# A recurrent attention and gated feed-forward kernel: conversions of the output weight queued behind the last masks and copies of part 1, leftover gate tiles in another form, and a fold's parts reordered

## The chip, the cores and the metric

The kernel runs on one core of a Trainium2 chip. The core has a matrix engine (TensorE, "PE" in the profile, with its weight loads listed apart as "PEld"), a vector engine (VectorE, "DVE"), a scalar engine (ScalarE, "ACT"), GpSimd ("POOL") and SyncE ("SP"), which here only issues DMA transfers. Each engine takes its own instructions strictly in order; they wait for each other through semaphores. The metric is the device time of one launch in microseconds. Before the change it is 488.24 us, the median of 4 runs (486.95 to 489.95). A difference under 0.5% (2.4 us) can't be told from no change with such runs.

## What is computed

The reference, cut to what matters: a gated linear attention over 4 batches, 8 heads, 768 steps and 48 values a head, and a feed-forward block on its output, where two projections are multiplied with each other.

```python
state = zeros((B, H, D, D)); y = zeros_like(q)
for t in range(S):
    state = alpha[:, :, t, :, None] * state + einsum('bhd,bhe->bhde', k[:, :, t], v[:, :, t])
    y[:, :, t] = einsum('bhd,bhde->bhe', q[:, :, t], state)
x = y.transpose(0, 2, 1, 3).reshape(B * S, H * D)      # 3072 x 384
a, b = x @ w1, x @ w2                                  # 384 -> 1024 each
out = (a * b @ w3) @ w_out                             # 1024 -> 1024 -> 384
```

The four weights arrive as 64-bit floating point, the four attention inputs and the result are 32-bit.

## The kernel before

**Part 1, the attention.** The sequence is cut into 24 chunks of 128 steps (`N = 24`), and the loop `for n in range(N + 1)` (line 568) handles one chunk in each turn, with its parts spread over neighbouring turns: decays (`logs`, `decays`), scaled and transposed queries and keys (`transposed`, whose copies out of PSUM are line 306 on ACT), the scores of a chunk and their causal mask (`scores`; the mask is line 347, two DVE instructions a chunk), the product with the carried state (`attend_state`, line 363), the product with the values (`attend`, line 369, with two ACT copies of the result in line 373), and the chunk's own outer product (`outer`, line 316 with a DVE addition in line 326). The result of a chunk goes to a buffer in HBM, `xd`, by the stores of line 241. Three chunks make a group of 384 columns; there are 8 groups.

**Gate tiles, which fill the matrix engine.** For a group `g` and a block `f` of 128 of the 1024 columns, `gate` computes both projections and multiplies them. Each number is split into three parts, so that one factor takes nine matmuls of 128x384: six of parts 0 and 1 into one PSUM bank, three of part 2. The group's input is fetched by `load_x` (line 384) and split into three parts by `split_x` (line 390 on ACT, lines 391 and 392 on DVE). There are two forms of a gate. The early form (`gate`, through `exact`) uses two banks for a factor, an ACT scaling (line 407) and a DVE combination (line 409), and a DVE product (line 445): for a tile two ACT and three DVE instructions. The late form (`late_gate`, through `onto`) uses one bank for a factor: six matmuls, an ACT scaling in place (line 422), and the last three matmuls on top of it, which `settle(2)` holds back until two more factors have begun; ACT then brings one factor out (line 454) and DVE multiplies (line 458): three ACT instructions and one DVE instruction for a tile. A tile's result is stored by line 469. The 24 early tiles of groups 0 to 4 are put into a list, `fill`, and handed out between the parts of the attention; those that part 1 leaves over are taken first by the second loop.

**Conversion of the weights.** `to_fp32` fetches one tile of raw 64-bit words by DMA (line 183, three buffers) and makes 32-bit numbers of it: on ACT lines 191 and 196, on DVE lines 192, 195, 198, 199 and 201. `load_gates` does so for the first two weights, `load_out` for the output weight (eight tiles of 128x384; further ACT lines 474 and 477, DVE lines 475 and 478), `load_w3` for the third weight (sixteen tiles of 128x512). A conversion is a generator that is advanced in steps by `convert`. In the last turns of part 1 the queue of conversions is refilled with those of the output weight (line 608), at `n == N - 1`.

**Part 2.** The loop `for i, x in enumerate(todo)` (line 635) goes over the leftover early tiles and then over the visits to (group, block range) in late form. Between tiles it advances the conversions by 2.2 steps (line 643). As soon as its memory is free, each turn also runs half of a `fold`: eight transposes of one block row of the third weight (line 495), its split into parts `h` (ACT, line 497), `l` and `m` (DVE, lines 498 and 499), for each half of the row, and 24 matmuls with the converted output weight, whose result `done` splits again (lines 504 to 506). There are eight folds. A last loop multiplies the stored gate tiles with the folded weight (`project`).

**Who sets the order.** The program is written in this order, but a scheduler orders each engine's queue by its own priorities before the launch. So an instruction that the source issues late may stand early in its engine's queue if its inputs are due early there.

Of the kernel before, what the change touches and what calls it, by code (L numbers as in the profile page):

```python
# [12 lines left out]
I32 = mybir.dt.int32  # L13
# [3 lines left out]
ALU = mybir.AluOpType  # L17
# [31 lines left out]
def kernel(  # L49
# [12 lines left out]
    nc = tc.nc  # L62
# [5 lines left out]
    N = B * NCH  # L68
# [102 lines left out]
    keep_bc = keep[:, None, :].to_broadcast([C, NP, C])  # L171
# [42 lines left out]
    weights, begun = deque(), deque()  # L214

    def fetch(ahead=3):
        while weights and len(begun) < ahead:
            begun.append(weights.popleft())
            next(begun[-1])

    def convert(steps, ahead=3):

        for _ in range(steps):
            fetch(ahead)
            if not begun:
                return
            x = begun.popleft()
            try:
                next(x)
                begun.appendleft(x)  # L230
            except StopIteration:
                pass
# [105 lines left out]
    def scores(n):  # L338
        qkT = st["qkT", n]
        sc = [bank().rearrange("p (j c) -> p j c", j=NP) for _ in range(2)]  # L340
        for j in range(NP):
            for i in range(2):
                r = ds(DP * i, D)
                nc.tensor.matmul(sc[i][:, j, :], qkT[r, 0, j, :], qkT[r, 1, j, :], start=True, stop=True)  # L344
        ms = work.tile([C, 2, NP, C], FP32, tag="ms", name="ms")
        for i in range(2):
            nc.vector.tensor_tensor(ms[:, i].bitcast(I32), sc[i].bitcast(I32), keep_bc, op=ALU.bitwise_and)  # L347
        st["ms", n] = ms

    HP = NP // 2  # L350
# [15 lines left out]
    def attend(n):  # L366
        (y, heads), ms, vc = st.pop(("y", n)), st.pop(("ms", n)), st.pop(("v", n))
        for j, i, to in heads:
            nc.tensor.matmul(to, vc[:, 2 * j + i, :], ms[:, i, j, :], start=(n % NCH == 0 and j % HP == 0),  # L369
                             stop=(j % HP == HP - 1), skip_group_check=True)  # L370
        x = work.tile([C, HP, 2, C], FP32, tag="x", name="x")
        for i in range(2):
            nc.scalar.copy(x[:, :, i], y[i])
        x = x.rearrange("p j i t -> p (j i) t")

        g, c = divmod(n, G)
        to = xd[g].rearrange("(b h d) t -> b d h t", b=2, d=D)
        for half in range(2):
            later.append((to[half, :, :, ds(c * C, C)], x[ds(DP * half, D)]))


    def load_x(g, queue=nc.sync):
        st["xT", g] = xp.tile([C, KM, TG], FP32, tag="xT", name="xT")
        queue.dma_start(out=st["xT", g], in_=xd[g].rearrange("(k p) t -> p k t", p=C))

    def split_x(g, i):
        x = st.pop(("xT", g))
        t = tr[i].tile([C, 3, KM, TG], FP32R, tag="x3", name="x3")
        st["x3", g] = t
        nc.scalar.activation(t[:, 0], x, AF.Copy, scale=1.0 - 2.0 ** -13)  # L390
        nc.vector.tensor_sub(t[:, 1], x, t[:, 0].bitcast(FP32))
        nc.vector.scalar_tensor_tensor(t[:, 2], t[:, 0].bitcast(FP32), -1.0 - 1.0 / P, x,  # L392
                                       op0=ALU.mult, op1=ALU.add)
# [14 lines left out]
        products(p2, w, x, (2,), n, True, True)  # L408
        nc.vector.scalar_tensor_tensor(to, p2, scale, t, op0=ALU.mult, op1=ALU.add)  # L409

    pending = deque()

    def settle(keep=0):

# [19 lines left out]
        return [([[w12[half][:, part, i, kk, ds(at, C)] for kk in range(KM)] for part in range(3)], x)  # L434
                for i in range(2)]

    def gate(g, f):
        r = []
        for factor, scale in zip(factors(g, f), (1.0, P * P)):
            r.append(gw.tile([C, TG], FP32, tag="r", name="r"))  # L440
            exact(r[-1], *factor, scale)
            if len(r) == 1:
                yield
        ab = abp.tile([C, TG], FP32, tag="ab", name="ab")
        nc.vector.tensor_mul(ab, *r)
        store_ab()
        st["ab"] = g, f, ab

    def late_gate(g, f):
        r = []  # L450

        def one(p):
            r.append(gw.tile([C, TG], FP32, tag="r", name="r"))
            nc.scalar.activation(r[0], p, AF.Copy, scale=P * P)

        def two(p):
            ab = abp.tile([C, TG], FP32, tag="ab", name="ab")
            nc.vector.tensor_mul(ab, p, r[0])  # L458
            store_ab()
            st["ab"] = g, f, ab  # L460

        for factor, done in zip(factors(g, f), (one, two)):
            onto(*factor, TG, done, 2)
            yield

    def store_ab():
        if "ab" in st:
            g, f, ab = st.pop("ab")
            nc.sync.dma_start(out=abd[g][:, f, :], in_=ab)
# [19 lines left out]
    def fold(i):  # L489
        w3 = st.pop(("w3", i))  # L490
        w3T = foldp.tile([C, 3, KF, C], FP32R, tag="w3T", name="w3T")
        for part in range(2):
            tp = bank().rearrange("p (j c) -> p j c", c=C)
            for j in range(KF // 2):
                nc.tensor.transpose(tp[:, j, :], w3[:, ds((part * KF // 2 + j) * C, C)], ident)  # L495
            h, l, m = (w3T[:, x, part * KF // 2:(part + 1) * KF // 2, :] for x in range(3))
            nc.scalar.activation(h, tp, AF.Copy, scale=1.0 - 2.0 ** -13)
            nc.vector.tensor_sub(l, tp, h.bitcast(FP32))  # L498
            nc.vector.scalar_tensor_tensor(m, h.bitcast(FP32), -1.0 - 1.0 / P, tp, op0=ALU.mult, op1=ALU.add)
        yield True  # L500

        def done(po):
            h, l, m = (w3o[:, part, i, :] for part in range(3))
            nc.scalar.activation(h, po, AF.Copy, scale=(1.0 - 2.0 ** -13) / P)
            nc.vector.scalar_tensor_tensor(l, h.bitcast(FP32), -P, po, op0=ALU.mult, op1=ALU.add)
            nc.vector.scalar_tensor_tensor(m, h.bitcast(FP32), P + 1.0, po, op0=ALU.mult, op1=ALU.subtract)

        onto(*([[x[:, part, j, :] for j in range(KF)] for part in range(3)] for x in (w3T, wo)), DM, done, 2)
# [59 lines left out]
    for n in range(N + 1):  # L568
        store()
        load_v(n + AHEAD - 1)  # L570
        load_a(n + 5)
        load_kq(n + AHEAD)
        if n:
            attend_state(n - 1)
        if n < N:
            scores(n)
        transposed(n + 1)
        if n - 2 in begin:
            g, tiles = begin[n - 2]
            split_x(g, 0)  # L580
            fill.extend(gate(g, f) for f in tiles)
        pieces = (0, 3, 3, 2)[(n - 6) % 4] if n > 5 else 0
        if n == 0:
            logs(2)
            decays(2)
            logs(3)
        early = n < 7
        if n < N:
            convert(1, 2 if n == 0 else 3)
        advance(n)  # L590
        if n:
            attend(n - 1)
        outer(n)
        run(pieces > 0)
        if early:
            convert(1)
        decayed(n + 2)
        logs(n + 4)
        if n in begin:
            load_x(begin[n][0])  # L600
        convert(early and n > 2)
        run(pieces > 1)
        decays(n + 3)
        if n < N:
            convert(early or n % 3 == 0)
        run(pieces > 2)
        if n == N - 1:
            weights.extend(load_out(j) for j in range(KF))
            fetch()
    store()  # L610
    part1.close()


    tr.append(pool("tr1", 1, reuse_waits="tile"))
# [9 lines left out]
    todo, order = list(fill), []  # L624
    low, high = range(FH), range(FH, KF)
    visits = [(5, low), (6, low), (7, range(KF))] + [(g, high) for g in (0, 1, 2, 3, 5, 6)]
    for k, (g, tiles) in enumerate(visits):
        order.append((max(len(todo) - 4, order[-1][0] + 1 if order else 0), len(todo), g, 1 - k % 2))
        todo += [late_gate(g, f) for f in tiles]
        if g == 7:  # L630
            halfway = len(todo) - len(high)
    owed = 0.0
    load_x(order[0][2])
    lastp = None
    for i, x in enumerate(todo):
        while order and i >= order[0][0]:
            split_x(*order.pop(0)[2:])
            if order:
                load_x(order[0][2])
        for _ in x:  # L640
            pass
        owed += 2.2
        convert(int(owed))
        owed -= int(owed)
        if i == halfway + 1:
            first.close()
            w3o = pool("w3op", 1, side="right", reuse_waits="tile").tile([C, 3, KF, DM], FP32R, name="w3o")
        if folded < KF:
            if w3o and folds and next(folds[0], None) is None:
                folds.popleft()  # L650
                folded += 1
        elif lastp is None:
            settle()
            folding.close()
            lastp = pool("lastp", 1, reuse_waits="tile")
            for n in range(4):
                load_ab(n)
# [40 lines left out]
```

## Time and profile before

| what | value |
|---|---|
| median of 4 runs | 488.24 us |
| the profiled execution, device time | 486.95 us |
| its span, first to last instruction | 485.1 us |
| PE busy | 457.8 us, 94% of the span |
| PEld busy | 432.7 us, 89% |
| DVE busy | 363.4 us, 75% |
| ACT busy | 274.3 us, 57% |
| POOL busy | 39.5 us, 8% |
| data moved by DMA | 80.30 MB, 166 GB/s over the span |
| granted clock of the matrix engine, mean | 0.989 |

The profiled execution's own time is 1.85 us above its span, which lies outside the first and last instruction. A "busy" share is an average over stages: in the first 80 us the matrix engine waits often, after that it is rarely idle. The first fold's transposes run at 254.8 us, the last one's at 336 us, and the last loop's first matmul at 380.5 us. In lists of waits, "idle before" is the time an engine stood still ahead of an instruction, and the name behind the arrow is the work whose end released it.

### The profile page before, as it was taken

What the parts mean: (1) busy time and instruction counts of PE and PEld (TensorE: products, weight loads), DVE (VectorE), ACT (ScalarE), POOL (GpSimd) and SP (SyncE); (2) the same over time, 40 slices, a digit from 0 to 9 for tenths busy, and PEclk for the clock granted to TensorE, in tenths of its full rate; (3) what the DMA queues carried; (4) which work ended last, traced back from release to release, by engine and by line L of the source; (5) the groups of instructions that cost most, each with busy time, mean ns of one, the idle gap of its engine ahead of it and who ended that gap; (6) DMA issues with size and microseconds to landing.
All of it is one profiled execution on the core that took longest, in us unless ns stands there. A gap on an engine that the chain in (4) does not pass through costs nothing.

```text
span 485.1 us, 9995 instructions
## 1 busy us (share of the span) xinstructions
PE 457.8 (94%) x3824; PEld 432.7 (89%) x3824; DVE 363.4 (75%) x592; ACT 274.3 (57%) x545; POOL 39.5 (8%) x83
## 2 busy tenths in 40 slices
PE   3798879999999999999999998999999999999997
PEld 1576669899898989999999996999999999999996
DVE  2679899997989687898987796893466366677671
ACT  2576667866767564568766664755446333333330
POOL 2133232112202200000000000000000000000000
PEclk9998799999999999999999999999999999999999
DMA  9999999999899965346573353321219445555511
GB/s 171 189 200 201 230 199 204 233 220 231 164 227 211 221 213 147 115 148 207 192 260 106 109 184 116 107 85 47 81 56 260 152 149 177 175 175 177 180 51 49
DMA packets 161296, 80.30 MB, mean 166 GB/s; under 512 B 104672, under 2 KB 155104, under 8 KB 161248
## 3 DMA queue, kind: packets, MB, share of 16 engines
q1 hardware_dynamic: 159968, 79.58, 64.9%
q8 instruction: 30, 0.49, 0.4%
q0 software_dynamic: 1280, 0.08, 0.4%
q14 instruction: 18, 0.15, 0.1%
HBM read 57.58 MB, written 22.06 MB: 164 GB/s over the span
## 4 chain that ended last, share of the span: by engine, by line
PE 75%; DVE 8%; DMA 7%; ACT 4%; issue 3%; SPq 2%; POOL 0%; ACTq 0%; DVEq 0%; POOLq 0%
PE bank L398 60%; DMA raw<-in_moe_w_dram 4%; PE bank L344 4%; PE bank L369 4%; PE bank L304 2%; PE bank L363 2%; PE bank L316 1%; DMA dec<-ends 1%; PE bank L495 1%; PE bank L269 1%; DVE x L392 1%; ACT x L390 1%; DMA ends<-e 1%; DVE power L199 1%; DMA raw<-in_moe_w_out_dram 1%
## 5 line engine op out<-in xcount | busy, mean ns | idle before, releaser
L398 PE MATMUL bank<-x,w 128*128 128x384 f32 x1152 | 211.6, 338 | 0.9 <-ACT bank L422 0.4
L398 PEld LDWEIGHTS bank<-x,w 128*128 128x128 f32 x1152 | 199.9, 188 | 3.6 <-ACT bank L422 1.3
L398 PE MATMUL bank<-w3o,ab 128*128 128x384 f32 x576 | 100.2, 336 | 0.0
L398 PEld LDWEIGHTS bank<-w3o,ab 128*128 128x128 f32 x576 | 99.9, 188 | 0.0
L407 ACT ACTIVATE t<-bank 128x384 f32<-128x384 f32 x72 | 35.1, 491 | 67.8 <-PE bank L398 67.5
L422 ACT ACTIVATE bank<-bank 128x384 f32<-128x384 f32 x88 | 41.9, 479 | 32.0 <-PE bank L398 31.8
L522 DVE TENSOR_TENSOR ab<-abl,ab 128x1024 fp32r<-128x1024 f32 x24 | 29.4, 1224 | 13.8 <-ACT ab L521 13.8
L398 PE MATMUL bank<-wo,w3T 128*128 128x384 f32 x192 | 36.9, 337 | 2.1 <-DVE w3T L498 1.1
L458 DVE TENSOR_TENSOR ab<-bank,r 128x384 f32<-128x384 f32 x40 | 22.1, 553 | 21.7 <-ACT bank L422 13.8
L521 ACT ACTIVATE ab<-abl 128x1024 fp32r<-128x1024 f32 x24 | 25.5, 1061 | 20.2 <-PE bank L398 18.8
L196 ACT ACTIVATE power<-power,rebias 128x512 uint32<-128x512 uint32 (+1 forms) x36 | 25.1, 700 | 20.3 <-DVE power L195 20.3
L344 PEld LDWEIGHTS bank<-qkT 48*128 48x128 f32 x384 | 26.1, 204 | 11.7 <-ACT qkT L306 4.0
L398 PEld LDWEIGHTS bank<-wo,w3T 128*128 128x128 f32 x192 | 33.2, 188 | 3.7 <-DVE w3T L498 2.1
L344 PE MATMUL bank<-qkT 48*128 48x128 f32 x384 | 31.1, 304 | 4.7 <-ACT qkT L306 2.8
L191 ACT ACTIVATE rest<-raw 128x512 f32<-128x512 uint32 (+1 forms) x36 | 23.4, 651 | 21.3 <-DMA raw<-in_moe_w_dram 15.5
L409 DVE SCALAR_TENSOR_TENSOR o<-bank,t 128x384 f32<-128x384 f32 x24 | 13.4, 558 | 27.4 <-issue 15.3
L409 DVE SCALAR_TENSOR_TENSOR r<-bank,t 128x384 f32<-128x384 f32 x48 | 26.5, 553 | 9.9 <-ACT t L407 5.1
L306 ACT COPY qkT<-bank 128x512 f32<-128x512 f32 x48 | 25.8, 586 | 13.0 <-PE bank L304 13.0
L347 DVE TENSOR_TENSOR ms<-bank,keep 128x512 int32<-128x512 int32 x48 | 31.1, 684 | 1.3 <-PE bank L344 1.2
L282 DVE TENSOR_TENSOR qk<-kq,e 128x768 f32<-128x768 f32 x24 | 22.9, 953 | 9.4 <-ACT e L273 8.9
L523 DVE SCALAR_TENSOR_TENSOR ab<-ab,abl 128x1024 fp32r<-128x1024 f32 x24 | 29.2, 1218 | 0.0
L369 PE MATMUL bank<-ms,v 128*64 128x128 f32 x384 | 28.0, 291 | 0.0
(73 smaller groups left out, 539.8 us busy)
## 6 DMA issues: line engine op xcount, KB each, us to landing
abd<-ab SPq DMA_DIRECT2D x64, 192.0 KB, 3.0
abl<-abd SPq DMA_DIRECT2D x24, 512.0 KB, 4.5
raw<-in_moe_w_dram SPq DMA_DIRECT2D x16, 512.0 KB, 4.7
xT<-xd SPq DMA_DIRECT2D x14, 576.0 KB, 4.0
raw<-in_moe_w_dram SPq DMA_DIRECT2D x24, 256.0 KB, 4.7
ac<-in_alpha_dram SPq DMA_DIRECT2D x24, 192.0 KB, 5.1
kq<-in_k_dram SPq DMA_DIRECT2D x24, 192.0 KB, 5.2
kq<-in_q_dram SPq DMA_DIRECT2D x24, 192.0 KB, 4.5
```

Source lines behind the costliest of these rows:

```text
L196: nc.scalar.activation(power, power, AF.Relu, scale=2.0 ** 23, bias=rebias)
L306: nc.scalar.copy(qkT[:, :, :, ds(DP * half, DP)], tp[half])
L344: nc.tensor.matmul(sc[i][:, j, :], qkT[r, 0, j, :], qkT[r, 1, j, :], start=True, stop=True)
L347: nc.vector.tensor_tensor(ms[:, i].bitcast(I32), sc[i].bitcast(I32), keep_bc, op=ALU.bitwise_and)
L369: nc.tensor.matmul(to, vc[:, 2 * j + i, :], ms[:, i, j, :], start=(n % NCH == 0 and j % HP == 0), stop=(j % HP == HP - 1), skip_group_chec ...
L398: nc.tensor.matmul(p, w[part][i], x[part][i], start=start and part == parts[0] and i == 0, stop=stop and part == parts[-1] and i == n - 1, ...
L407: nc.scalar.activation(t, p1, AF.Copy, scale=(1.0 + 1.0 / P) * scale)
L409: nc.vector.scalar_tensor_tensor(to, p2, scale, t, op0=ALU.mult, op1=ALU.add)
L422: nc.scalar.activation(p, p, AF.Copy, scale=1.0 + 1.0 / P)
L521: nc.scalar.activation(t[:, 0], ab, AF.Copy, scale=1.0 - 2.0 ** -13)
L522: nc.vector.tensor_sub(t[:, 1], ab, t[:, 0].bitcast(FP32))
L523: nc.vector.scalar_tensor_tensor(t[:, 2], t[:, 0].bitcast(FP32), -1.0 - 1.0 / P, ab, op0=ALU.mult, op1=ALU.add)
```

## The change

It has three parts. In the first, the conversions of the output weight are put into the queue of conversions at `n == N - 3`, that is at step 21, after all conversions of the first two weights have been advanced to their end; turns 22 and 23 of part 1 no longer advance any. The DVE and ACT instructions of the conversions and of `split_x` that the second loop issues are placed, by `tc.issue_after`, behind the last mask of part 1 on DVE and behind its last copy on ACT. DMA transfers, which SP issues, get no such order. In the second part, `gate` chooses its form only when a tile is begun, so that the tiles left over from part 1 are made in late form. In the third, a fold computes both halves' `h` and `l` before both halves' `m`.

```diff
-            nc.vector.tensor_tensor(ms[:, i].bitcast(I32), sc[i].bitcast(I32), keep_bc, op=ALU.bitwise_and)
+            masked = nc.vector.tensor_tensor(ms[:, i].bitcast(I32), sc[i].bitcast(I32), keep_bc, op=ALU.bitwise_and)
+        ends_of_part1[0] = masked.ins
...
-            nc.scalar.copy(x[:, :, i], y[i])
+            copied = nc.scalar.copy(x[:, :, i], y[i])
+        ends_of_part1[1] = copied.ins
...
-    pending = deque()
+    ends_of_part1 = [None, None]
+    pending, late = deque(), False
...
-    def gate(g, f):
+    def early_gate(g, f):
...
+    def gate(g, f):
+        yield from (late_gate if late else early_gate)(g, f)
...
         w3T = foldp.tile([C, 3, KF, C], FP32R, tag="w3T", name="w3T")
+        rest = []
         for part in range(2):
...
             nc.scalar.activation(h, tp, AF.Copy, scale=1.0 - 2.0 ** -13)
             nc.vector.tensor_sub(l, tp, h.bitcast(FP32))
+            rest.append((m, h, tp))
+        for m, h, tp in rest:
             nc.vector.scalar_tensor_tensor(m, h.bitcast(FP32), -1.0 - 1.0 / P, tp, op0=ALU.mult, op1=ALU.add)
...
-        if n < N:
+        if n < N - 2:
             convert(1, 2 if n == 0 else 3)
...
-        if n < N:
+        if n < N - 2:
             convert(early or n % 3 == 0)
         run(pieces > 2)
-        if n == N - 1:
+        if n == N - 3:
+            while begun:
+                convert(1)
             weights.extend(load_out(j) for j in range(KF))
             fetch()
     store()
     part1.close()
+    late = True
...
-        todo += [late_gate(g, f) for f in tiles]
+        todo += [gate(g, f) for f in tiles]
...
-        while order and i >= order[0][0]:
-            split_x(*order.pop(0)[2:])
-            if order:
-                load_x(order[0][2])
+        with tc.issue_after(ends_of_part1[0]), tc.issue_after(ends_of_part1[1]):
+            while order and i >= order[0][0]:
+                split_x(*order.pop(0)[2:])
+                if order:
+                    load_x(order[0][2])
         for _ in x:
             pass
         owed += 2.2
-        convert(int(owed))
+        with tc.issue_after(ends_of_part1[0]), tc.issue_after(ends_of_part1[1]):
+            convert(int(owed))
```

## The prediction

> **What bounds the kernel now.** The page first, then the busy time by stretches: the matrix engine works almost without a gap from 80 us on, except in the turn from part 1 to part 2 and among the folds.
>
> ```profile
> PE 457.8 (94%) x3824; PEld 432.7 (89%) x3824; DVE 363.4 (75%) x592; ACT 274.3 (57%) x545; POOL 39.5 (8%) x83
> ```
>
> ```profile
> 180.00:200.00 20.00, 19.08 (x163) 17.74 (x162) 16.82 (x31) 11.31 (x26) 0.00 (x0) 1.00 0.40 116
> ...
> 200.00:220.00 20.00, 20.00 (x116) 20.00 (x115) 18.91 (x40) 12.74 (x28) 0.00 (x0) 1.00 0.49 165
> ...
> 280.00:300.00 20.00, 18.48 (x105) 17.16 (x103) 15.19 (x27) 12.81 (x27) 0.00 (x0) 1.00 0.44 141
> 300.00:320.00 20.00, 19.05 (x111) 18.69 (x112) 17.95 (x33) 11.37 (x22) 0.00 (x0) 1.00 0.32 100
> ```
>
> (After the stretch and its length: PE, PEld, DVE, ACT, POOL, clock, DMA.) No matmul is removed, so only gaps can be won. The timelines show two places. At the turn, the matmuls of chunk 22 wait for the mask L347, which stands behind conversions and a split on DVE:
>
> ```profile
> 179.97 0.43 PE L363 MATMUL bank<-qkT,T 48*64 48x128 f32 x4
> 181.29 0.65 PE L363 MATMUL bank<-qkT,T 48*64 48x128 f32 x12 [0.89 <-DVE ms L347]
> ```
>
> ```profile
> 178.35 0.55 DVE L201 TENSOR_TENSOR mant<-mant,power 128x384 f32<-128x384 f32 x1
> 178.81 0.55 DVE L445 TENSOR_TENSOR ab<-r 128x384 f32<-128x384 f32 x1
> 179.28 1.35 DVE L391 TENSOR_TENSOR x<-xT,x 128x1152 fp32r<-128x1152 f32 x1
> 180.55 1.28 DVE L347 TENSOR_TENSOR ms<-bank,keep 128x512 int32<-128x512 int32 x2
> ```
>
> In the fourth fold:
>
> ```profile
> 296.56 0.80 PE L398 MATMUL bank<-x,w 128*128 128x384 f32 x3 [0.43 <-ACT bank L422]
> 298.12 1.66 PE L398 MATMUL bank<-wo,w3T 128*128 128x384 f32 x8 [0.76 <-ACT w3T L497]
> 300.90 0.97 PE L398 MATMUL bank<-wo,w3T 128*128 128x384 f32 x4 [1.12 <-DVE w3T L498]
> 301.71 0.34 PE L398 MATMUL bank<-x,w 128*128 128x384 f32 x1
> 302.10 0.96 PE L398 MATMUL bank<-wo,w3T 128*128 128x384 f32 x4
> ```
>
> ```profile
> 295.47 0.66 ACT L191 ACTIVATE rest<-raw 128x512 f32<-128x512 uint32 x1 [1.85 <-DMA raw<-in_moe_w_dram]
> 296.03 0.47 ACT L422 ACTIVATE bank<-bank 128x384 f32<-128x384 f32 x1
> 296.44 1.14 ACT L390 ACTIVATE x<-xT 128x1152 fp32r<-128x1152 f32 x1
> 297.49 1.06 ACT L497 ACTIVATE w3T<-bank 128x512 fp32r<-128x512 f32 x2
> ```
>
> The second place is what matters: ACT stood at L191 until raw words landed, and L422, L390 and L497, which PE wanted, queued behind. Followed back, those words were requested at 290.58, when DVE's L199 gave a buffer back; DVE was late because ACT's L191 at 283.50 had waited for a load of 278.98; before that DVE ran without a gap from 269.51, where it waited for L504, behind an L191 that waited for a load of 264.16; DVE before that without a gap from 258.38, where it waited for L497 behind an L191 fed by a load of 251.83. So from 251.8 to 302 one chain of DVE, raw load and ACT runs beside PE and at last overtakes it. All PE gaps after 176 us: 0.89, 0.11 (at 287.87), 0.43, 0.76, 1.12, and, within the folds' 24 matmuls, about 0.33 (at 272.38, by the weight loads) and 0.45 (300.90 to 302.90 holds nine matmuls that need 9 x 0.172 = 1.55). Sum **4.1 us**: the most that this change can win.
>
> [...] PEld's idle at the same places is 1.13+0.33+0.43+0.75+1.09+1.44+0.37 = 5.5. I take 4.1, from matmul starts: a weight load may be late while earlier matmuls still drain.
>
> **The masks (part one, DVE).** In the built order of the changed kernel 16 conversion instructions leave DVE ahead of the last mask (seven L192/L195 starting 0.27 apart, nine others 0.47: 6.1 us) and ten L191/L196 leave ACT (about 4.8). But both halves of the split, L391 and L392, now stand ahead of chunk 22's mask. ACT's L390 can't overwrite the old split before PE's 18 matmuls from 172.99 end at 176.38; then 1.17 for L390, 1.27 each for L391 and L392 (start to start), the mask starts at 180.15 instead of 180.55, and PE resumes at 180.87. **Gain 0.42 of the 0.89.** Nothing is late next: the second half of this mask and the last chunk's end by 184.0 (186.94 before).
>
> **The leftover tiles (part two).** Five tiles change form: ten L409 (554 ns) and five L445 (554) go, five L458 (550) come. DVE loses ten instructions, 10 x 0.47 = 4.7 us; ACT gains five, 5 x 0.41 = 2.0. PE's order moves by one matmul in all. ACT has room (12.7 of 20 us at 200 to 220), but the form is tighter: in the early form only a bank waits for ACT; now the last three matmuls wait for L422. They come 18 matmuls after the first six, 18 x 0.177 = 3.2 us (64.19 us for 363 matmuls, 190.60 to 254.79), less 0.47 for L422: **2.7 us of patience**. Behind L422's neighbours L196 and L474 ACT waits for DVE; walking both queues with the trace's durations, the nearest call is 0.9 us (group 5's third tile, its last L422 behind an L191 on the first third-weight load). Cost 0, at worst 3 (first rival below).
>
> **The conversion's clock.** After the first fold DVE's and ACT's orders are the same in both kernels but for the fold's own swap, so what counts is when the chain enters the folds. Take the sixth third-weight L199, whose end sends the load of 251.83. Before: from the last mask's end, 186.94, to its start, 251.12, is 64.2 us; by start-to-start times (0.27/0.335, 0.47, 0.60, 1.27) the instructions between hold 56.6, so DVE idled 7.6. After: 57.9 us of work (+6.1 moved in, -4.7 saved), from 184.0. With the same idle time it starts at 249.5, **1.6 us earlier**; with the walk's 6.1 us at 248.0, **3.1 earlier**. The walk: DVE first waits for ACT's L191 until 191.3, behind the last copy L373, then meets waits of under 1 us; the eighth output-weight tile's L478 runs near 226.8 (232.88 before), the first third-weight product near 230.8 (233.82). At the first fold the lead is cut by PE: L458 ahead of the fold needs matmuls ending at 254.4, so L498 starts at 256.0 instead of 258.38, and the L458 that ran at 277.72 has a lead of about 2.2. **I take 2.2** (between 1.6 and 2.4); bounds -0.5 and +3.1.
>
> SP's queue: loads one to three keep their places (168.6 to 172), since three buffers bound them; "from step 21" moves nothing there. Loads four to eight move behind the last `xd` stores, the fourth to about 192.4, after L199 frees a buffer, the next ones 3 to 7 us apart. Behind them wait only tile stores with three buffers. [...] The row: such a load lands in 3.8 us. [...]
>
> **The fold's swap (part three).** The second L498 no longer follows the first L499: it comes 0.60 sooner, `m` as much later and still long before its use (302.6 against 305.88). The gap at 302.10 closes: **0.45**; that at 272.38 too, 0.33, which counts only as far as the chain isn't what ends last.
>
> **The sum.** In the fourth fold the first L498 ends at 300.84 - 2.2 = 298.64; nine matmuls later PE is at 300.2 instead of 302.90. The gain is **2.2 + 0.45, about 2.7 us**; of it 0.42+0.33+0.11+0.43 and most of 0.76 are gaps gone, and what stays is PE waiting some 1.2 us for L498. After it no gap stood before, and the chain is still 2.2 early where PE is 2.7 early, 0.5 us of slack used. Against its own 486.95 (span 485.1 and 1.85 outside) the profiled execution would take 484.3; it is the lowest of the four runs, so the median goes from 488.24 to **485.5 us**, -0.55%.[...]
>
> **Rivals.**
> - *The fourth fold's wait vanishes wholly.* With a lead of 3.1 or a load landing in 3.9 instead of 4.8 us: gain about 3.6, **484.6**. For: loads land in 3.0 to 6.0. Against: PE holds the lead at 2.4. Chance 0.12.
> - *The chain keeps its time.* Waits of DVE on ACT and loads, now strung one behind the other, use up the lead: gain 0.45 alone, **487.8**. For: 7.6 us of idle DVE in this stretch before, of which I assume 1.5 less. Against: five tiles lighter. Chance 0.25.
> - *Slower: ACT blocked in late form.* Nine late tiles in a row meet the output weight's conversion. A tile is 3.1 us of DVE against 3.2 of PE, so each added idle us on DVE stays; L196 and L474 hold L422 behind them. It decides from DVE idling 12 us instead of 6: 2.7 us late uses the patience, and the folds come 3 us late; 488.24 + 3 - 0.45 = **490.8**. For: at 241.17 L458 ran 2.3 us behind its matmuls, and the printed chain passes from L422 to PE at 243.03. Against: no stall came of it. Chance 0.13.
>
> The forecast has 0.50, its own range 484.5 to 487.0; two thirds of it lies beyond 0.5%. Faster: 0.33 + 0.12 = 0.45; same: 0.17 + 0.25 = 0.42; slower: 0.13. The range 484.0 to 489.0 leaves out the slower rival and little else.
>
> **What would show it.** L363 of chunk 22 waiting about 0.5 us for the mask; 38 L409 and 45 L458 in their counterparts; the first fold's L498 near 256; the fourth fold's waits for L422 and L497 gone, that for L498 near 1.2; no x1 between the `l` matmuls. Wrong if L422 gaps appear between 195 and 250, or the first fold's L498 comes at 258 or later.

## The result, and the profile after

The changed kernel takes **485.67 us** (median of 43 runs, 482.40 to 491.48) against 488.68 us for the kernel before (64 runs, 484.66 to 492.68). The ratio is **0.9946, 95% interval 0.9931 to 0.9962**: 1.9 to 3.4 us less, 2.6 in the middle. The forecast was 485.5 us. The profiled execution took 483.91 us with a span of 482.1. It looks like a prediction that came true, and it is one in the total only. The profile, and above all further profiles of both kernels, show the time coming from another place than the one I had named.

In the changed kernel line 347 is still the mask; L363 has become L364 and L369 L370, the split L390/391/392 is L392/393/394, the matmuls of L398 are L400, L422 is L425, L458 is L461, and of the fold L497/498/499 are L504/505/508. First the page (engine, busy time, share, instructions):

```profile
PE 453.8 (94%) x3824; PEld 430.5 (89%) x3824; DVE 358.2 (74%) x582; ACT 276.2 (57%) x550; POOL 38.7 (8%) x83
```

The five tiles have changed form as counted: ten instructions fewer on DVE, five more on ACT. Next the turn from part 1 to part 2, matrix engine and DVE:

```profile
178.86 0.67 PE L364 MATMUL bank<-qkT,T 48*64 48x128 f32 x16
179.88 1.16 PE L344 MATMUL bank<-qkT 48*128 48x128 f32 x16 [0.35 <-DVE ms L347]
```

```profile
176.50 1.36 DVE L393 TENSOR_TENSOR x<-xT,x 128x1152 fp32r<-128x1152 f32 x1
177.78 1.35 DVE L394 SCALAR_TENSOR_TENSOR x<-x,xT 128x1152 fp32r<-128x1152 f32 x1
179.05 1.28 DVE L347 TENSOR_TENSOR ms<-bank,keep 128x512 int32<-128x512 int32 x2
```

As forecast, both halves of the split stand ahead of the mask, and no step of a conversion does. The wait of 0.89 us has become 0.35, and it stands at L344 now: all 16 matmuls of L364 run before it. Then the fourth fold, on PE and ACT:

```profile
293.93 0.79 PE L400 MATMUL bank<-x,w 128*128 128x384 f32 x3 [0.39 <-ACT bank L425]
295.49 1.66 PE L400 MATMUL bank<-wo,w3T 128*128 128x384 f32 x8 [0.77 <-ACT w3T L504]
298.27 1.66 PE L400 MATMUL bank<-wo,w3T 128*128 128x384 f32 x8 [1.12 <-DVE w3T L505]
299.77 3.28 PE L400 MATMUL bank<-x,w 128*128 128x384 f32 x18
```

```profile
292.83 0.66 ACT L191 ACTIVATE rest<-raw 128x512 f32<-128x512 uint32 x1 [1.85 <-DMA raw<-in_moe_w_dram]
293.40 0.48 ACT L425 ACTIVATE bank<-bank 128x384 f32<-128x384 f32 x1
293.81 1.15 ACT L392 ACTIVATE x<-xT 128x1152 fp32r<-128x1152 f32 x1
294.86 1.06 ACT L504 ACTIVATE w3T<-bank 128x512 fp32r<-128x512 f32 x2
```

The eight `l` matmuls are one row, so the swap's gap is closed. The three waits that were to go or to shrink are still there, 0.39, 0.77 and 1.12 against 0.43, 0.76 and 1.12, behind an L191 that stands for the same 1.85 us as before. The lead of the conversion, which was to bring 2.2 of the 2.7 us, can't be seen where it was to pay. A new wait has come too, 0.33 us for L425 at 252.23, where ACT stands behind two L191 of the third weight.

### The profile page after: what moved, and what is told of

Its sections match the earlier page's. It is cut to its first block, busy times and chain, and to the rows that moved or that the text cites. A ratio compares the mean times of both kernels' runs of the same rounds, so it can differ in the third digit from the quotient of the medians.

```text
span 482.1 us, 9979 instructions
## 1 busy us (share of the span) xinstructions
PE 453.8 (94%) x3824; PEld 430.5 (89%) x3824; DVE 358.2 (74%) x582; ACT 276.2 (57%) x550; POOL 38.7 (8%) x83
## 4 chain that ended last, share of the span: by engine, by line
PE 73%; DVE 12%; DMA 6%; ACT 3%; issue 3%; SPq 2%; POOL 0%; DVEq 0%; POOLq 0%; ACTq 0%
PE bank L400 61%; DMA raw<-in_moe_w_dram 4%; PE bank L344 3%; PE bank L370 3%; DVE ms L347 1%; PE bank L364 1%; PE bank L304 1%; DVE x L394 1%; DVE power L199 1%; DMA dec<-ends 1%; PE bank L502 1%; DVE qk L282 1%; DVE x L393 1%; DVE w L212 1%; DMA ends<-e 1%
## 5 line engine op out<-in xcount | busy, mean ns | idle before, releaser
L400 PE MATMUL bank<-x,w 128*128 128x384 f32 x1152 | 211.2, 338 | 1.1 <-ACT bank L425 0.7
L400 PEld LDWEIGHTS bank<-x,w 128*128 128x128 f32 x1152 | 199.7, 188 | 3.7 <-issue 1.4
L400 PE MATMUL bank<-w3o,ab 128*128 128x384 f32 x576 | 100.2, 336 | 0.0
L400 PEld LDWEIGHTS bank<-w3o,ab 128*128 128x128 f32 x576 | 99.9, 188 | 0.0
L409 ACT ACTIVATE t<-bank 128x384 f32<-128x384 f32 x62 | 30.3, 491 | 64.5 <-PE bank L400 64.3
L425 ACT ACTIVATE bank<-bank 128x384 f32<-128x384 f32 x98 | 46.7, 478 | 34.2 <-PE bank L400 33.4
L461 DVE TENSOR_TENSOR ab<-bank,r 128x384 f32<-128x384 f32 x45 | 24.9, 554 | 23.2 <-ACT bank L425 13.3
L400 PE MATMUL bank<-wo,w3T 128*128 128x384 f32 x192 | 36.3, 335 | 1.9 <-DVE w3T L505 1.1
L400 PEld LDWEIGHTS bank<-wo,w3T 128*128 128x128 f32 x192 | 33.4, 188 | 2.5 <-DVE w3T L505 1.4
L344 PEld LDWEIGHTS bank<-qkT 48*128 48x128 f32 x384 | 25.6, 203 | 10.8 <-ACT qkT L306 4.3
L344 PE MATMUL bank<-qkT 48*128 48x128 f32 x384 | 30.4, 302 | 4.5 <-ACT qkT L306 3.2
L191 ACT ACTIVATE rest<-raw 128x512 f32<-128x512 uint32 (+1 forms) x36 | 23.3, 648 | 18.6 <-DMA raw<-in_moe_w_dram 18.6
L347 DVE TENSOR_TENSOR ms<-bank,keep 128x512 int32<-128x512 int32 x48 | 31.1, 682 | 2.3 <-PE bank L344 2.3
L411 DVE SCALAR_TENSOR_TENSOR r<-bank,t 128x384 f32<-128x384 f32 x38 | 21.0, 553 | 10.7 <-ACT t L409 7.6
L370 PE MATMUL bank<-ms,v 128*64 128x128 f32 x384 | 27.4, 287 | 0.0
```

Source lines behind the costliest of these rows:

```text
L347: masked = nc.vector.tensor_tensor(ms[:, i].bitcast(I32), sc[i].bitcast(I32), keep_bc, op=ALU.bitwise_and)
L400: nc.tensor.matmul(p, w[part][i], x[part][i], start=start and part == parts[0] and i == 0, stop=stop and part == parts[-1] and i == n - 1, ...
L409: nc.scalar.activation(t, p1, AF.Copy, scale=(1.0 + 1.0 / P) * scale)
L425: nc.scalar.activation(p, p, AF.Copy, scale=1.0 + 1.0 / P)
```

## Reading single profiles: a common anchor

The two spans differ by 3.0 us, but 1.16 of them arise before the turn: the last group of 18 gate matmuls ahead of the turn starts at 172.99 before and at 171.83 after. Over all profiles of this study that start lies between 171.78 and 176.67, in no relation to what was changed. So I measure each profile from that start. "Turn" is the time from there to part 2's first matmul, "part 2" from that matmul to the end of the span, "fold 4" from the first transpose of the fourth fold to the 18 matmuls behind its `l`. The same matmuls lie between these points in all kernels. "Mask" is the start of chunk 22's L347, from the same anchor. The runs e1 to e12 are told of below.

| profile | order at the end of part 1 | raw buffers | mask | turn | part 2 | fold 4 |
|---|---|---|---|---|---|---|
| before | no | 3 | 7.56 | 17.61 | 294.50 | 10.41 |
| e10, before again | no | 3 | 9.02 | 20.65 | 294.05 | 10.77 |
| e3, before with the swap | no | 3 | 8.01 | 18.10 | 294.78 | 11.20 |
| e9, before with 4 buffers | no | 4 | 9.67 | 21.19 | 290.03 | 6.96 |
| after | yes | 3 | 7.22 | 16.67 | 293.60 | 9.89 |
| e8, after again | yes | 3 | 7.17 | 16.70 | 296.72 | 11.21 |
| e2, after without the order | no | 3 | 8.09 | 18.47 | 292.26 | 8.42 |
| e1, early leftovers | yes | 3 | 7.19 | 16.72 | 295.62 | 11.12 |
| e4, no swap | yes | 3 | 7.19 | 16.72 | 293.96 | 10.52 |
| e12, order alone | yes | 3 | 7.23 | 16.67 | 296.14 | 10.10 |
| e6, L394 behind the fold's parts | yes | 3 | 7.22 | 16.75 | 295.06 | 11.41 |
| e5, after with 4 buffers | yes | 4 | 7.19 | 16.64 | 289.99 | 6.77 |
| e7, 4 buffers and L394 behind | yes | 4 | 7.17 | 16.62 | 289.99 | 6.77 |
| e11, 4 buffers, mask ahead of the split | yes | 4 | 5.13 | 16.25 | 289.93 | 6.77 |

Two things stand out. **Where the order is set, the turn is the same in every profile**, 16.62 to 16.75 us (16.25 where the mask is moved as well); without it, it lies anywhere from 17.61 to 21.19. And **part 2 with three buffers scatters from 292.3 to 296.7 us**, while with four buffers it is 289.93 to 290.03 whatever else is changed.

What sets the mask's time can be read as well. In the profiles without the order, DVE works without a gap, e9 aside, from the first step (L192) on the output weight's second raw tile up to the mask, and that step waits for a load. DVE in the first profile of the kernel before, and in e10:

```profile
175.00 0.36 DVE L192 TENSOR_SCALAR mant<-raw 128x384 uint32<-128x384 uint32 x1 [1.21 <-DMA raw<-in_moe_w_out_dram]
```

```profile
176.07 0.36 DVE L192 TENSOR_SCALAR mant<-raw 128x384 uint32<-128x384 uint32 x1 [1.98 <-DMA raw<-in_moe_w_out_dram]
```

In every profile this load is requested 1.76 to 1.81 us ahead of the anchor, and it lands 3.76 to 6.40 us later. **Without the order the mask follows the landing at a fixed distance**, 5.57 to 5.58 us in the first profile, e10, e3 and e2. (In e9 it is 6.47, because another L192 stands ahead there and DVE waits 0.53 us for ACT.) With the order, and step 22's split left in its place, the load takes 3.91 to 6.40 us, and the mask starts at 7.17 to 7.23 all the same. So the order takes a DMA load out of the mask's way.

## The experiments

Each was timed together with the kernel before, on one chip; what follows "Measured" is the ratio to it with its 95% interval. Each profile is that of one execution. The runs with four buffers have 6 or 7 timed executions, the others 22.

**e1, the form of the leftover tiles.** `late` is never set, and part 2's visits call the late form directly.

```diff
-    late = True
-        todo += [gate(g, f) for f in tiles]
+        todo += [late_gate(g, f) for f in tiles]
```

> The changed kernel with its five leftover tiles back in the early form; the order behind part 1's ends and the swap stay. Theory A (the gain is the lead with which the chain of DVE, raw loads and ACT enters the folds, and the lighter form pays for most of it): DVE has ten instructions or about 4.7 us more between 190 and 250 us, the first fold's tensor_sub of l starts 1.5 to 4 us later against the turn than in the changed kernel (255.5 there), the fourth fold's waits for w3T grow by about as much; ratio to the kernel before 0.998 to 1.003. Theory B (the masks' order at the turn and the swap carry the gain, the form of the tiles does not matter): the folds' waits stay as in the changed kernel, ratio 0.993 to 0.996.

Measured: 0.9961 [0.9939, 0.9983]. The ratio lies between the two ranges, and its interval touches both. The conversion is indeed later, as theory A says: the sixth third-weight L199 starts 64.48 us after part 2's first matmul, against 58.86 in the changed kernel. But the first fold's `l` (L505) starts 66.69 after it, against 67.02: 5.6 us of delay are gone within one fold. Part 2's 295.62 us lie inside the scatter of the changed kernel (293.60 and 296.72), so what DVE lost can't be found at PE, as theory B says.

**e2, no order.** Both blocks that queue conversion and splits behind part 1's last mask and copy are taken out.

```diff
-        with tc.issue_after(ends_of_part1[0]), tc.issue_after(ends_of_part1[1]):
-            while order and i >= order[0][0]:
+        while order and i >= order[0][0]:
...
-        with tc.issue_after(ends_of_part1[0]), tc.issue_after(ends_of_part1[1]):
-            convert(int(owed))
+        convert(int(owed))
```

> The changed kernel without the two blocks that keep conversion and splits behind part 1's last mask and copy; the fetch at step 21, the late form and the swap stay. Theory A: the conversion is free to stand ahead of the last masks again, so the waits at the turn grow from 0.4 to about 0.9 us or more, while the chain enters the folds about as early as in the changed kernel; ratio 0.995 to 0.998. Theory B (the order is what carries the gain): the turn and the folds are back at the kernel before's; ratio 0.999 to 1.002.

Measured: 0.996 [0.9934, 0.9986]; theory A's numbers. Its turn:

```profile
183.50 0.66 PE L364 MATMUL bank<-qkT,T 48*64 48x128 f32 x12 [1.39 <-DVE ms L347]
184.49 1.16 PE L344 MATMUL bank<-qkT 48*128 48x128 f32 x16 [0.34 <-ACT qkT L306]
```

Waits for the mask and for a copy sum to 1.7 us, 1.4 more than with the order. Part 2 is the shortest of all with three buffers, and the conversion stands 7 us earlier (sixth L199 51.76 after part 2's start). Of these 7 us, 0.9 is left at the first fold's `l`, which can't run before PE's transposes, and 1.4 at the fourth fold's. **The order takes 1.8 us out of the turn and, in this pair of profiles, gives 1.3 back in part 2.**

**e3 and e4, the swap alone and the change without it.** e3 puts the loop `for m, h, tp in rest` into the kernel before; e4 takes it out of the changed kernel.

```diff
+            rest.append((m, h, tp))
+        for m, h, tp in rest:
             nc.vector.scalar_tensor_tensor(m, h.bitcast(FP32), -1.0 - 1.0 / P, tp, op0=ALU.mult, op1=ALU.add)
```

> The kernel before with the fold's swap alone. Theory A: the gap among the fourth fold's eight l matmuls closes, 0.4 us (and perhaps 0.3 in the second fold), everything else stays: ratio 0.998 to 1.000. Theory B (each fold's l comes 0.6 us sooner and this adds up over the folds that wait): 1 to 2 us, ratio 0.996 to 0.998.

> The changed kernel without the fold's swap. Theory A: the l matmuls of the fourth fold come in two groups of four again with a gap of 0.4 us between them; ratio 0.9945 to 0.9965, 0.1% above the changed kernel's. Theory B (the swap adds up over folds): 1 to 2 us above the changed kernel, ratio 0.997 to 0.999.

Measured: e3 1.0005 [0.9981, 1.0029], e4 0.9972 [0.9947, 0.9997]. e3 lies just above theory A's range and e4 in theory B's, but a tenth of a percent is less than these intervals resolve. The trace does resolve it. In e4:

```profile
299.22 0.98 PE L400 MATMUL bank<-wo,w3T 128*128 128x384 f32 x4 [1.12 <-DVE w3T L504]
300.04 0.34 PE L400 MATMUL bank<-x,w 128*128 128x384 f32 x1
300.41 0.97 PE L400 MATMUL bank<-wo,w3T 128*128 128x384 f32 x4
301.22 3.11 PE L400 MATMUL bank<-x,w 128*128 128x384 f32 x17
```

Nine matmuls take 2.00 us instead of 9 x 0.172 = 1.55: the 0.45 is there with the old order and gone with the new one (in e3 as in the changed kernel the eight are one row). It does not add up over folds: part 2 is 0.3 us longer in e3 than in the kernel before and 0.4 us longer in e4 than in the changed kernel, both less than two profiles of one kernel differ.

**e5, four raw buffers.** If the folds are late because raw words are requested only when DVE gives a buffer back, a fourth buffer cures it.

```diff
-    rawp = pool("rawp", 3, stack=conversion, side="right")
+    rawp = pool("rawp", 4, stack=conversion, side="right")
-            convert(int(owed))
+            convert(int(owed), 4)
```

> The changed kernel with four raw buffers instead of three, and four conversions begun ahead in part 2. Theory A (the fourth fold is late because raw words are requested only when DVE gives a buffer back, and ACT stands at L191 until they land): L191's waits of 1.6 and 1.9 us before the fourth fold go, and with them PE's 0.39 for L425 and 0.77 for L504, the 0.33 at 252 us too; 1.0 to 2.5 us less than the changed kernel, ratio to the kernel before 0.990 to 0.993. Theory B (DVE's own work sets the fourth fold's time): the waits stay, ratio as the changed kernel's, 0.9946.

Measured: 483.00 us, **0.9871 [0.9822, 0.9920]**. Theory A, and more than it asked for: the wait of 1.12 us, which I had thought separate, goes too. The fourth fold, PE:

```profile
294.92 3.37 PE L400 MATMUL bank<-x,w 128*128 128x384 f32 x18
298.13 2.93 PE L400 MATMUL bank<-wo,w3T 128*128 128x384 f32 x16
300.90 3.28 PE L400 MATMUL bank<-x,w 128*128 128x384 f32 x18
```

No row has a wait, and the 6.77 us from transposes to the next group are 42 matmuls one behind the other, at a granted clock of 1.00 (292 to 304 us). After 160 us L191's waits for third-weight words sum to 2.3 us, against 14.7 in the changed kernel.

**e6 and e7, the split.** In the fourth fold DVE runs L393 and L394 ahead of L505. Asking for this one split a tile later moves just L394 behind L505 and L508 in the built order; e7 adds the fourth buffer.

```diff
-        order.append((max(len(todo) - 4, order[-1][0] + 1 if order else 0), len(todo), g, 1 - k % 2))
+        order.append((max(len(todo) - (3 if k == 5 else 4), order[-1][0] + 1 if order else 0), len(todo), g, 1 - k % 2))
```

> The changed kernel with the split before the fourth fold asked for one tile later, which in the built order moves one instruction: L394 stands behind the fold's L505 and L508 on DVE instead of ahead of them. Theory A (the fourth fold's wait of 1.12 us for L505 is DVE's 1.27 us of L394, put ahead of what PE needs): the 1.12 goes, the waits for L425 and L504 stay (0.4 and 0.8); ratio 0.991 to 0.9935. Theory B (L505 waits for the raw loads' chain whatever stands ahead of it, or L394 is then late for its tiles): the time is the changed kernel's or more, ratio 0.9945 to 0.997.

> Four raw buffers and L394 behind the fold's parts together. If the two waits are separate, as theory A has it, the fourth fold runs without a wait over 0.2 us and the time is 2.0 to 2.7 us below the changed kernel's: ratio 0.9885 to 0.9905. If one stall stands behind both, the gain is that of the better one alone, ratio 0.991 to 0.993.

Measured: e6 0.9952 [0.9930, 0.9975], e7 0.9894 [0.9846, 0.9941]. In e6 the wait for L505 is gone, as theory A says, and the time is not better. Two rows show why: L191 waits longer in this profile (2.91 us instead of 1.85), so PE waits 1.74 for L425; and 16 matmuls then need 4.62 us.

```profile
296.95 0.80 PE L400 MATMUL bank<-x,w 128*128 128x384 f32 x3 [1.74 <-ACT bank L425]
298.51 4.62 PE L400 MATMUL bank<-wo,w3T 128*128 128x384 f32 x16 [0.76 <-ACT w3T L504]
```

```profile
296.00:299.00 3.00, 1.29 (x6) 0.97 (x7) 0.99 (x1) 3.00 (x6) 0.00 (x0) 1.00 0.00 0
299.00:302.00 3.00, 3.00 (x12) 3.00 (x11) 3.00 (x6) 1.11 (x3) 0.00 (x0) 0.53 0.00 0
```

(Busy time by stretch: PE, PEld, DVE, ACT, POOL, then the granted clock.) After a stretch in which PE was busy 1.29 of 3 us, its clock was 0.53 for the next 3: 3 x 0.47 = 1.4 us lost on top of the waits. e7's ratio lies in the range that I had put down for two separate waits, and its interval covers both ranges; the profile decides. Its part 2 and fold 4 equal e5's to 0.01 us. So one stall stands behind all three waits, the raw loads; moving L394 is worth nothing once it is gone.

**e8 and e10, both kernels again**, unchanged, for another profile each.

> The changed kernel itself, with another profile: how much of what a profile shows is chance. Theory A: the waits at the turn and in the fourth fold are the same within 0.3 us (the orders of all queues are fixed), and what differs between profiles lies in part 1's first 70 us, several us; ratio 0.993 to 0.9965. Theory B (the lead into the folds is itself chance): the fourth fold's waits differ by more than 0.5 us.

> The kernel before itself, with another profile. The turn takes 17.6 to 18.5 us (0.9 to 1.4 us of it for the mask); the fourth fold's waits sum to 2.3 us if its raw words land in 4.9 us and to about 3.6 us if they land in 6.2; ratio 0.998 to 1.002.

Measured: e8 0.9964 [0.9936, 0.9992], e10 1.0013 [0.9990, 1.0035]. The turn of the changed kernel is the same to 0.03 us, its folds are not. The fourth fold of e8, PE and ACT:

```profile
298.97 0.79 PE L400 MATMUL bank<-x,w 128*128 128x384 f32 x3 [1.70 <-ACT bank L425]
300.53 1.66 PE L400 MATMUL bank<-wo,w3T 128*128 128x384 f32 x8 [0.77 <-ACT w3T L504]
303.31 1.66 PE L400 MATMUL bank<-wo,w3T 128*128 128x384 f32 x8 [1.12 <-DVE w3T L505]
```

```profile
297.88 0.66 ACT L191 ACTIVATE rest<-raw 128x512 f32<-128x512 uint32 x1 [3.13 <-DMA raw<-in_moe_w_dram]
```

That load was requested at 291.70 and used at 297.88, 6.18 us later; in the first profile it was 287.91 to 292.83, 4.92. The same load takes 4.9 to 5.3 us in six profiles with three buffers and 6.2 to 6.5 in four (e1, e3, e6, e8), with the same requests around it at the same times, and the difference goes straight to PE. Theory B was right for the folds. e8 also has a wait that the first profile showed small, 1.18 us for L425 at 255.09, just ahead of the first fold. e10's turn was to take 17.6 to 18.5 us, with 0.9 to 1.4 of it for the mask, and takes 20.65, with 1.66. The first profile's turn was the shortest of the four with the old order (before, e3, e9, e10). In e10:

```profile
182.36 0.65 PE L363 MATMUL bank<-qkT,T 48*64 48x128 f32 x12 [1.66 <-DVE ms L347]
183.05 1.40 PE L344 MATMUL bank<-qkT 48*128 48x128 f32 x16
184.38 1.97 PE L369 MATMUL bank<-ms,v 128*64 128x128 f32 x16
```

```profile
180.00:184.00 4.00, 2.30 (x43) 1.80 (x40) 4.00 (x5) 2.06 (x5) 0.00 (x0) 0.98 0.56 186
184.00:188.00 4.00, 4.00 (x28) 3.44 (x26) 3.97 (x11) 2.13 (x5) 0.00 (x0) 0.59 0.66 187
```

The mask comes 1.5 us later against PE than in the first profile, as the load behind its queue lands 1.5 us later, and DVE is busy for all of the 4 us around it. Then the clock is 0.59 for four microseconds, and L369 takes 1.97 us instead of 1.09: another 1.6 us.

**e9, four buffers without the change.**

```diff
-    rawp = pool("rawp", 3, stack=conversion, side="right")
+    rawp = pool("rawp", 4, stack=conversion, side="right")
-        convert(int(owed))
+        convert(int(owed), 4)
```

> The kernel before with four raw buffers and four conversions begun ahead in part 2, and nothing of the change. Theory A (what the folds lose is set by the raw loads alone, so that the buffer does what the change's lead was to do): the fourth fold runs without a wait, from part 2's first matmul to the end 290.0 to 290.6 us as in the changed kernel with four buffers (294.5 before); the turn stays at 17.6 to 18.5; ratio 0.990 to 0.993. Theory B (the lighter form and the order are needed too): the fourth fold still waits over 1 us, ratio 0.993 to 0.997.

Measured: 483.43 us, **0.9905 [0.9868, 0.9942]**. Part 2 is at the floor without order, form or swap. What is left of the change is the turn alone: 21.19 us here, 16.64 in e5, though the times of e9 and e5 differ by less than their intervals resolve. The turn was to stay at 17.6 to 18.5, and this missed. It shows the same pattern as e10, L363's wait and then a clock of 0.60 (184 to 188 us):

```profile
182.19 0.65 PE L363 MATMUL bank<-qkT,T 48*64 48x128 f32 x12 [2.28 <-DVE ms L347]
183.88 1.97 PE L369 MATMUL bank<-ms,v 128*64 128x128 f32 x16
```

**e11, the rest of the turn.** On top of e5, step 22's split is queued behind that step's mask.

```diff
-            split_x(g, 0)
+            with tc.issue_after(ends_of_part1[0]) if g == 4 else ExitStack():
+                split_x(g, 0)
```

> The changed kernel with four raw buffers, and the split of step 22 queued behind that step's mask. Theory A (both halves of the split ahead of the mask are what is left of the turn's wait): the mask starts about 2.5 us earlier, the 0.35 us for it goes, the turn takes 16.3 us (16.65 in the changed kernel), part 2 stays at 290.0; ratio 0.986 to 0.990. Theory B (the split is then late for its tiles): a wait for the split appears ahead of the first L400 of its group, ratio 0.989 to 0.993.

Measured: **480.69 us, 0.9845 [0.9810, 0.9880]**. DVE at the turn:

```profile
179.35 1.29 DVE L347 TENSOR_TENSOR ms<-bank,keep 128x512 int32<-128x512 int32 x2 [0.46 <-PE bank L344]
180.56 1.35 DVE L393 TENSOR_TENSOR x<-xT,x 128x1152 fp32r<-128x1152 f32 x1
```

Now DVE waits for PE there and not PE for DVE; the 0.35 is gone, and from 160 us on no wait of PE is left that the view of waits lists. It is the fastest version of the study, with the lowest median, though its interval overlaps that of e5.

**e12, the order alone**, which is e1 and e4 together: early leftovers, no swap, but the order and the fetch at step 21.

> The order behind part 1's ends and the later fetch alone: leftover tiles in early form, no swap. Theory A' (formed on the runs so far: the order's fixed turn carries most of the gain, and form and lead bring nothing that outlasts the raw loads): the turn takes 16.6 to 16.75 us with 0.35 for the mask, as in every profile with the order, against 17.6 to 21.2 without; part 2 takes 294 to 297 us, as before; ratio 0.995 to 0.9975. Theory B' (form and swap carry it): the turn is the same, but part 2 is 2 us or more longer than before's 294.3, and the ratio is 0.999 or above.

Measured: 487.71 us against 490.27, **0.9952 [0.9931, 0.9972]**, in the range of theory A': with the turn at 16.67, and part 2 no better than before, the order alone brings what the whole change brings, within the intervals. Part 2, 296.14, is near what theory B' asked for, 2 us above the kernel before's; the ratio is not. Here too PE waits for L425 ahead of the first fold, 1.24 us at 254.39.

## Why the prediction was right, and where it was not

**The total** was right, 485.5 against 485.67. The profiled execution was to take 484.3 and took 483.91; but 1.16 us of its gain lies ahead of the turn, where the sum had nothing.

**The masks: right about what waits, wrong in size, and this is the main error.** "Gain 0.42 of the 0.89" takes the one turn that I had for the kernel's turn. The after side was exact: the mask was to start at 180.15, which is 7.16 from the anchor, and starts at 7.22. The before side was the best of four: its mask starts at 7.56, 8.01, 9.02 or 9.67, by when the second raw tile lands, and I had seen DVE's instructions ahead of the mask but not the load at their head. With the order DVE has idle time ahead of the split (1.45 and 1.02 us in e8), so PE sets the mask's time. The turn takes 19.39 us on average in the four profiles with the old order and 16.69 in the eight with the new one, e11 aside: **2.7 us**, of which about 0.8 comes from the lowered clock after the two long waits (1.6 us each in e9 and e10, shared among four profiles). Without e9, whose queue differs, it is 2.1. An estimate from more loads agrees: over all 14 profiles the load takes 4.72 us on average, so that the old mask would start at 4.72 - 1.78 + 5.58 = 8.5 and, as in the two profiles whose clock stays at 1.00 there (before and e3), the turn end 10.1 later, at 18.6; that is 1.9 us more than 16.69, and the lowered clock comes on top. In the first pair alone the turn gained 0.94. A second, smaller reason is that L364's 16 matmuls no longer wait for the mask: only L344 does.

The turn alone is thus about as large as the measured gain of 1.9 to 3.4 us, from a step that I had booked at 0.42. Part 2 adds nothing that shows: with three buffers it averages 295.2 us in the six profiles with the order and 294.4 in the three of the kernel before and e3. From the anchor to the end these profiles take 311.9 against 313.2, a gain of 1.3; part 2 differs by 3.1 between two profiles of the changed kernel, so they can't place the gain more closely. That the total came out as forecast was luck: the 2.2 us of the lead did not come, and the turn paid about as much more than booked.

**The leftover tiles: right as a cost, not as a source.** No stall for L425 came between 195 and 250 us in the first profile. Ahead of the first fold there is one of 0.33 us, and of 1.18 in e8; e12, with leftover tiles in early form, has 1.24, so the late form does not explain it. The 4.7 us that DVE saves can't be seen at PE (e1).

**The conversion's clock: this step failed.** "I take 2.2" counted the lead on the trace's clock, while a wait of PE shrinks only by the lead over PE, and PE was to be earlier itself. Counted from part 2's first matmul, the sixth L199 comes at 60.52, 60.07, 58.90 and 58.89 without the change, at 58.86 and 58.70 with it: a lead of 0 to 1.8. At the first fold even that is lost: L498 at 67.78, 67.51, 67.04 (65.54 with a fourth buffer) against L505 at 67.02 and 68.79. In the fourth fold it is 109.56, 110.13 and 109.11 against 109.03 and 112.09. On the trace's clock the first fold's L505 comes at 255.5 in the first profile, as forecast, but at 259.3 in e8, beyond the 258 that was to be the sign of an error. Each link of the chain waits for a load which the link before requests, and a lead becomes waiting there: the waits of L191 for third-weight words sum to 14.7 and 17.2 us with the change, against 12.2 to 13.9 in the kernel before and e3. Only a far larger lead, the 7 us of e2, left something: its waits of L191 sum to 8.5 us, and 1.4 us is left of the lead at the fourth fold. The forecast that the waits for L422 and L497 would be gone was wrong; the rival "the chain keeps its time" describes part 2. Its time, 487.8, missed, and the turn's gain is what it lacked.

**The swap: right**, 0.45 in the trace. As a time of its own it could not be measured.

**The slower rival** did not come. What loads four to eight cost can't be told from the rest of the order, without which the conversion stood 7 us earlier (e2); no wait of PE shows it.

**The two sums weighed.** The most that this change could win was put at 4.1 us from matmul starts, 5.5 by the weight loads' idle time. From the anchor to the end, the first profile has 312.11 us, e11, without waits, 306.18: **5.9**. The weight loads' idle time came nearer, and I went against it. For the output weight's loads, requested later, no loss showed at PE; for the third weight's loads, of which I said only that they set a chain, requesting one buffer earlier is worth 4.0 to 4.8 us of part 2 (290.03 in e9 against 294.05 to 294.78).

What stays open: why the same load lands after 3.8 us in one execution and 5.2 or 6.4 in another at the turn, and after 4.9 or 6.2 in the fourth fold. And the times alone do not separate e1, e2, e4, e6, e8 and e12; the split of the gain rests on the profiles, five without the order at the turn and nine with it.

## What to carry to other kernels

Look at several profiles of the kernel before, set to a common anchor, before sizing a wait: follow each wait back to what started the work ahead of it. Here the wait that went back to the landing of a load varied between executions (the load took 3.76 to 6.40 us, the wait 0.89 to 2.28), one that went back to PE's own matmuls did not (0.35 us, the mask at 7.17 to 7.23), and removing the varying one was worth its mean, about 2.7 us of the turn, not the 0.94 of one pair of profiles. A lead counts only against the engine that waits, and little of it outlived a chain whose every link waits for a load that the link before requests (1.4 of the 7 us in e2); there, another buffer was worth more than an earlier start (4.0 to 4.8 us of part 2). And when two or three waits stand in a row, ask first whether one late transfer is behind them all.

## What the runs showed of the hardware

A wait of PE cost more than its length where the granted clock fell after it. In the first profile of the kernel before the clock is 0.50 from 41.83 to 45.25 us, which loses 1.7, and again from 52.07 to 58.90; in that of the changed kernel from 33.34 to 36.76 and from 50.41 to 57.24. From 165 to 460 us it fell in three of the profiles, each time by about 1.7 us in all (in e10 0.02 of the 4 us from 180 and 0.41 of the next 4). Behind other waits it stayed at 1.00:

| profile | stretch with the wait, us | PE busy in it, us | granted clock behind it |
|---|---|---|---|
| e9, turn | 179.50 to 182.90 | 1.12 of 3.40 | 0.60 (184 to 188) |
| e6, fourth fold | 296.00 to 299.00 | 1.29 of 3.00 | 0.53 (299 to 302) |
| e10, turn | 180.30 to 183.70 | 1.70 of 3.40 | 0.59 (184 to 188) |
| e2, turn | 181.70 to 185.10 | 1.67 of 3.40 | 1.00 (184 to 192) |
| e3, turn | 182.60 to 186.00 | 2.02 of 3.40 | 1.00 (184 to 192) |
| e1, fourth fold | 296.00 to 300.00 | 1.67 of 4.00 | 1.00 (300 to 308) |
| e8, fourth fold | 296.00 to 300.00 | 2.06 of 4.00 | 1.00 (300 to 308) |

The stretches of e10 and e2, nearly equal:

```profile
180.30:183.70 3.40, 1.70 (x29) 1.25 (x29) 3.40 (x5) 1.97 (x5) 0.00 (x0) 1.00 0.52 181
```

```profile
181.70:185.10 3.40, 1.67 (x28) 1.18 (x28) 3.40 (x4) 2.06 (x5) 0.00 (x0) 1.00 0.43 160
```

PE was busy for the same time to 0.03 us, and only e10 lost the 1.7. So the busy time of such a stretch does not tell by itself which wait costs clock, and what does is not shown. A part of the difference between nearly equal waits in two executions is this clock.
